# Placing the rows of the last step but one with a selection matrix, and masking the key sums in one instruction, in a four-layer attention kernel

## The chip, the core and the metric

The kernel runs on one core of a Trainium2 chip. A core has five instruction queues that run side by side and meet only at semaphores: TensorE (PE, matrix products into PSUM), VectorE (DVE), ScalarE (ACT), GpSimd (POOL, which here mostly issues DMA transfers) and SyncE (SP, which issues the others). The metric is the device time of one execution in microseconds, the median of the runs. All times below are microseconds unless marked ns.

## What is computed

The reference applies four blocks to a sequence x of 2048 tokens with 512 features, each on a layernorm of x and added back to x: A, B, A, B, with the same weights each time. Cut to what matters:

```python
def A(x, mem):                       # 64 segments of 32 tokens, one after the other
    for s in range(64):
        h = concat([mem, x[32*s:32*s+32]])       # 8 memory rows + 32 tokens
        q, k, v = h @ Wq, h @ Wk, h @ Wv         # 32 heads of 128
        p = softmax(where(mask, q @ k.T * scale, -1e9))
        o = (p @ v) @ Wo
        mem = o[:8]                              # goes into the next segment
        out.append(o[8:])
def B(x):                            # linear attention, 32 heads of 16
    q, k, v = split(x @ wqkv)
    phi = lambda t: where(t > 0, t + 1, exp(t)) + 1e-6
    kv, z = phi(k).T @ v, phi(k).sum(tokens)     # over all 2048 tokens
    return (phi(q) @ kv) / (phi(q) @ z + 1e-6) @ wo
x = x + A(ln(x)); x = x + B(ln(x)); x = x + A(ln(x)); x = x + B(ln(x))
```

A is a recurrence: the 8 memory rows that a segment puts out are an input of the next. B needs the sums kv and z over all tokens before its first output, so the next A layer, or the end of the kernel, waits for the last tokens of the A layer before.

## The kernel before

**Tiles and steps.** Tokens lie in 16 tiles of 128 rows, each covering four segments. A segment is a step; there are 64 steps in a layer, each with its projections (`kq0`, `kq1`, `v`), the memory rows' attention (`mem0`, `mem1`), the product with Wo of the memory rows and the tokens of the step before (`out`, L1386), the memory rows for the next step (`next`) and the tokens' attention (`x`). A step handles 8 memory rows and only the first 24 of its 32 tokens; the last 8 tokens of each of a tile's four segments, 32 rows, are gathered into a fifth block, the left-over rows (`left0` to `lefts`, and `left_rows`, L1443).

**From the output product to x.** `out_proj` leaves the two feature halves of a step's result in the rows of one PSUM tile; two 128-column casts (ACT or DVE, L937 or L938) put part of it into `outW_sb`. `rows_out` (L1432) adds the two partial results into `y_sb` (L1435, DVE, 64x256) and moves the rows to their places in `dx_sb` by DMA, two transfers per group of rows, issued on POOL (L953). When a tile's four steps are there, `residual` (L1447) adds `dx_sb` to x (L1474). For the very last step of a layer (tile 15, g = 3) there is another way: a product with the selection matrix `selz_sb` (L1458, two matmuls) puts the rows of `outW_sb` into place in PSUM, and DVE adds them to x (L1462).

**B, spread over A.** `b_in` (L1545) runs on each finished tile of x: layernorm (L1097 to L1111; ACT does the logarithm and exponential between L1098 and L1103), the products with wqkv, phi (exponential on ACT L1539, then DVE L1540 and L1542), and the sums kv (L1582) and z (L1584). The tokens' x and phi(q) go to scratch in DRAM. After the last tile, `b_mid` (L1599) masks kv to the heads' diagonal blocks (L1604), makes the masked key sums `zf_sb` by four multiplications (L1608), and multiplies kv into wo, in place. `b_out` (L1642) then gives a tile's output: a product with `zf_sb`, reciprocal by logarithm and exponential on ACT (L1667, L1669), a multiplication (L1670), the product with the mixed weights and the addition to x (L1679). In layer 0 tile 0's `b_out` stands ahead of the next A layer's first projection and the others run among its steps; in layer 1 all sixteen stand at the end, and SP stores them.

**The order of the work.** Every operation is recorded with the data that it reads and writes. A table written out in the kernel gives each a number and, where ACT or DVE could do it, the engine: `PERIOD` holds four steps that repeat, `OWN` the steps that differ (the first eleven and the last ones of each layer, the first eight of layer 1, and all of the end). `schedule` (L698) sorts by these numbers, gives out the eight PSUM banks in that order, and derives the semaphore waits. The numbers only set an order; each engine runs its own instructions strictly in it. While PE has nothing to do, `spin` (L1069) has it multiply ones.

## Time and profile before

| what | value |
|---|---|
| three runs, median (lowest to highest) | 1611.34 (1610.76 to 1618.56) |
| the profiled execution | 1611.15 |
| its span | 1609.4 |
| PE busy in the span | 1544.0 (96%) |
| DVE busy | 1221.6 (76%) |
| ACT busy | 1100.0 (68%) |
| POOL busy | 326.8 (20%) |
| granted PE clock, mean | 0.998 |
| first weights there and first projection starts | 25.64 |
| last tile of layer 0: its layernorm starts | 789.11 |
| first projection of layer 1 starts | 805.10 |
| last tile of layer 1: its layernorm starts | 1576.52 |

The span runs from the first to the last record of the trace; the device time also covers what lies around it. An engine's busy time is the sum over its instructions, and instructions of one engine can overlap by some tens of nanoseconds, so that ten DVE operations of 0.68 in a row take 0.60 each on the chain. The chain is followed back from the last instruction, at each step to what released it. "issue" is time in which the engine waited for nothing that the profile shows.

### The profile page before, as it was taken

What the parts mean: (1) busy time and instruction counts of PE and PEld (TensorE: products, weight loads), DVE (VectorE), ACT (ScalarE), POOL (GpSimd) and SP (SyncE); (2) the same over time, 40 slices, a digit from 0 to 9 for tenths busy, and PEclk for the clock granted to TensorE, in tenths of its full rate; (3) what the DMA queues carried; (4) which work ended last, traced back from release to release, by engine and by line L of the source; (5) the groups of instructions that cost most, each with busy time, mean ns of one, the idle gap of its engine ahead of it and who ended that gap; (6) DMA issues with size and microseconds to landing.
All of it is one profiled execution on the core that took longest, in us unless ns stands there. A gap on an engine that the chain in (4) does not pass through costs nothing.

```text
span 1609.4 us, 104163 instructions
## 1 busy us (share of the span) xinstructions
PE 1544.0 (96%) x52074; PEld 882.0 (55%) x43376; DVE 1221.6 (76%) x3899; ACT 1100.0 (68%) x3178; POOL 326.8 (20%) x660
## 2 busy tenths in 40 slices
PE   5899999999999999999999999999999999999997
PEld 1455555555555555555545655556556555555554
DVE  3777777887777787777677778777787877877777
ACT  1567776776776776776467777777777777776665
POOL 2022221122222112222201221222221222221120
PEclk9999999999999999999999999999999999999999
DMA  9300000000000000000000000000000000000013
GB/s 381 104 14 16 14 17 10 16 17 17 17 14 17 10 17 16 17 17 17 25 8 11 17 20 20 20 14 17 21 17 20 21 20 11 21 17 22 24 43 130
DMA packets 35079, 50.96 MB, mean 32 GB/s; under 512 B 13624, under 2 KB 28784, under 8 KB 33104
## 3 DMA queue, kind: packets, MB, share of 16 engines
q0 software_dynamic: 21744, 19.78, 4.3%
q1 hardware_dynamic: 12736, 24.38, 4.1%
q8 instruction: 374, 6.13, 1.6%
q14 instruction: 65, 0.53, 0.1%
q10 hardware_dynamic: 160, 0.14, 0.0%
HBM read 29.63 MB, written 10.49 MB: 25 GB/s over the span
## 4 chain that ended last, share of the span: by engine, by line
PE 85%; DVE 5%; ACT 5%; DMA 2%; issue 1%; POOL 0%; DVEq 0%; SPq 0%
PE pb L1157 27%; PE pb L1053 22%; PE pb L1400 17%; PE pb L1065 11%; ACT arena_sb L937 3%; PE pb L1049 3%; PE pb L1424 2%; DMA Wq_sb<-in_A_Wq_dram 2%; PE pb L1258 2%; DVE arena_sb L938 1%; PE pb L1338 1%; PE pb L1111 1%; DVE st_sb L1097 1%; DMA dx_sb<-y_sb 1%; DVE Wq_sb L1679 1%
## 5 line engine op out<-in xcount | busy, mean ns | idle before, releaser
L937 ACT ACTIVATE arena_sb<-pb 128x512 bf16<-128x512 f32 (+5 forms) x1140 | 521.0, 488 | 273.5 <-PE pb L1053 165.2
L953 POOL DMA_DIRECT2D dx_sb<-y_sb x504 | 254.6, 511 | 1047.7 <-DVE y_sb L1435 822.3
L1157 PE MATMUL pb<-Wk_sb,arena_sb 128*32 128x512 bf16 x4096 | 408.5, 379 | 3.0 <-DVE arena_sb L938 1.4
L1053 PE MATMUL pb<-Wq_sb,arena_sb 128*32 128x512 bf16 x4096 | 408.1, 379 | 0.0
L938 DVE CAST arena_sb<-pb 128x512 bf16<-128x512 f32 (+3 forms) x576 | 311.5, 545 | 110.9 <-PE pb L1053 57.9
L1400 PE MATMUL pb<-Wo_sb,arena_sb 128*32 128x256 bf16 x10368 | 345.3, 273 | 4.3 <-DVE arena_sb L1307 1.7
L1065 PE MATMUL pb<-arena_sb 128*32 128x128 bf16 (+2 forms) x12528 | 321.7, 216 | 4.2 <-ACT arena_sb L937 1.5
L1065 PEld LDWEIGHTS pb<-arena_sb 128*32 128x32 bf16 x12528 | 227.7, 96 | 138.1 <-issue 28.5
L1175 DVE STREAM_TRANSPOSE arena_sb<-arena_sb 128x256 f32<-128x256 f32 x640 | 260.9, 429 | 42.8 <-ACT arena_sb L937 36.6
L1400 PEld LDWEIGHTS pb<-Wo_sb,arena_sb 128*32 128x32 bf16 x10368 | 263.1, 96 | 50.6 <-issue 15.7
L1157 PE MATMUL pb<-Wv_sb,arena_sb 128*32 128x512 bf16 x3248 | 279.6, 378 | 1.1 <-DVE arena_sb L938 1.1
L1157 PEld LDWEIGHTS pb<-Wk_sb,arena_sb 128*32 128x32 bf16 x4096 | 119.4, 96 | 237.5 <-issue 186.2
L1053 PE MATMUL pb<-Wv_sb,arena_sb 128*32 128x512 bf16 x1872 | 202.8, 378 | 0.0
L937 ACT ACTIVATE arena_sb<-arena_sb 32x256 bf16<-32x256 bf16 (+1 forms) x414 | 159.6, 386 | 31.3 <-DVE arena_sb L1345 21.4
L1157 PEld LDWEIGHTS pb<-Wv_sb,arena_sb 128*32 128x32 bf16 x3248 | 95.9, 96 | 73.6 <-issue 19.2
L937 ACT ACTIVATE outW_sb<-pb 128x128 fp32r<-128x128 f32 x317 | 70.3, 273 | 89.2 <-PE pb L1400 86.2
L1307 DVE TENSOR_TENSOR arena_sb<-pb,arena_sb 128x128 bf16<-128x128 f32 x252 | 73.1, 290 | 50.5 <-PE pb L1400 17.2
L1157 PE MATMUL pb<-Wq_sb,arena_sb 128*32 128x512 bf16 x1024 | 101.6, 378 | 4.5 <-DMA Wq_sb<-in_A_Wq_dram 3.4
L1275 ACT ACTIVATE arena_sb<-pb 128x192 bf16<-128x192 f32 (+1 forms) x256 | 83.9, 328 | 31.2 <-PE pb L1258 12.7
L1435 DVE TENSOR_TENSOR y_sb<-pb,outW_sb 64x256 bf16<-64x256 f32 x158 | 65.8, 417 | 47.6 <-ACT outW_sb L937 44.2
L1053 PE MATMUL pb<-Wk_sb,arena_sb 128*32 128x512 bf16 x1024 | 101.7, 378 | 0.0
L1285 DVE TENSOR_TENSOR arena_sb<-arena_sb 128x128 bf16<-128x128 bf16 x504 | 89.0, 215 | 15.9 <-ACT arena_sb L1275 14.1
(109 smaller groups left out, 1793.0 us busy)
## 6 DMA issues: line engine op xcount, KB each, us to landing
Wk_sb<-in_A_Wk_dram SPq DMA_DIRECT2D x1, 4096.0 KB, 13.2
Wq_sb<-in_A_Wq_dram SPq DMA_DIRECT2D x1, 4096.0 KB, 24.3
Wv_sb<-in_A_Wv_dram SPq DMA_DIRECT2D x1, 4096.0 KB, 33.8
Wo_sb<-in_A_Wo_dram SPq DMA_DIRECT2D x16, 256.0 KB, 7.3
xs_scratch<-x_sb POOLq DMA_DIRECT2D x32, 128.0 KB, 2.0
pq_scratch<-arena_sb POOLq DMA_DIRECT2D x32, 128.0 KB, 2.9
dx_sb<-y_sb POOLq DMA_DIRECT2D x252, 12.0 KB, 1.6
dx_sb<-y_sb POOLq DMA_DIRECT2D x252, 4.0 KB, 1.9
```

Of the source, the lines that this page charges most:

```text
L937: return e.activation(o() if callable(o) else o, i() if callable(i) else i, ACTF.Copy)
L938: return e.tensor_copy(o() if callable(o) else o, i() if callable(i) else i)
L953: add(eng, lambda e: e.dma_start(o, i), 0.55 if eng == "pool" else 0.4, reads=reads, writes=writes, dsem="%s%d" % (kind, k), lat=lat + (0. ...
L1053: return pe.add_instruction(mybir.InstMatmult(name=nc.get_next_instruction_name(), engine=mybir.EngineType.PE, ins=[pe.lower_ap(x), pe.low ...
L1065: r = pe.matmul(o[q], w[:, q], x, start=start, stop=stop, skip_group_check=True, tile_position=(0, 32 * j))
L1157: r = pe.matmul(o, blk[:, c, :], w, start=(c == 0), stop=(c == 3), tile_position=(0, 32 * j))
L1175: add("dve", lambda v: v.transpose(dst, src(img[:, k, :].bitcast(F32))), 0.445, reads=[("img", k)], writes=[dkey])
L1275: add("act", lambda a: a.activation(PQ[:, r2, b, 0:nq], tl.f32()[:, 0:nq], ACTF.Exp, scale=SCALE), c_act(nq), tiles=[tl], writes=[("PQ", r ...
L1285: add("dve", lambda v, a=a, p_=p_, w_=w_: v.tensor_tensor(wide(Pm[:, k, a, :]), p_.unsqueeze(2).to_broadcast([128, 4, 4, 8]), w_, ALU.mult ...
L1307: add("dve", lambda v: v.tensor_tensor(oTb[:, s % NO, 16 * b:16 * b + 16, 0:8], pv.f32()[:, 0:128].rearrange("p (n q) -> p n q", q=8), Rm[ ...
L1400: r = pe.matmul(tl.f32()[32 * j:32 * j + 32, 0:256], oT[:, 4 * hh + n, :], Wo_sb[:, 8 * n + hh, 256 * d:256 * d + 256], start=(hh == 0 and ...
L1435: add("dve", lambda v: v.tensor_tensor(y_sb[0:64, k, :], tl.f32()[0:64, 0:256], outW[64:128, w, :].bitcast(F32), ALU.add), c_dve(256), rea ...
```

## The change

Four things change in the code. The selection matrix has four blocks of 32 columns instead of two of 128, made by four more selects in the set-up: two blocks pick a step's rows into places 0 to 31, two skip the 8 memory rows and pick 24 rows into places 0 to 23. The rows of tile 15's last step but one (g = 2) go through a product with it, as those of the last step do, and both additions to x touch 32 rows instead of 128. Since the left-over rows still come through `dx_sb`, POOL first sets its rows 64 to 95 to zero. And the four multiplications of the masked key sums become one with both operands spread out.

```diff
-    selz_sb = sb("selz_sb", [128, 2, 128], F32R)
+    selz_sb = sb("selz_sb", [128, 4, 32], F32R)
...
-        o = 16 + 128 * d
-        sel(scr_sb[q, o + 96:o + 128], ALU.not_equal, 1.0, 0, [[-1, 32]], 1, *SCR)
+        o = 16 + 32 * d
+        sel(scr_sb[q, o:o + 32], ALU.not_equal, 1.0, 0, [[-1, 32]], 1, *SCR)
+        sel(scr_sb[q, o + 64:o + 88], ALU.not_equal, 1.0, -8, [[-1, 24]], 1, *SCR)
...
-            if G == NT - 1 and g == 3:
+            if G == NT - 1 and g == 2:
+                add("pool", lambda p: p.memset(dx_sb[64:96, G % 2, :], 0.0), 0.5, writes=[("dx", G % 2, i, d) for i in (64, 88) for d in range(2)])
+            if G == NT - 1 and g >= 2:
                 tz = P.tile()
+                r = slice(32 * g, 32 * g + 32)
 
                 def pick(pe):
                     for d in range(2):
-                        r = pe.matmul(tz.f32()[:, 256 * d:256 * d + 256], selz_sb[:, d, :], outW[:, w, :], start=d == 0,
+                        u = pe.matmul(tz.f32()[0:32, 256 * d:256 * d + 256], selz_sb[:, d + 6 - 2 * g, :], outW[:, w, :], start=d == 0,
                                       stop=d == 1, skip_group_check=True)
-                    return r
+                    return u
                 add("pe", pick, 0.42, reads=[("outW", w, 0), ("outW", w, 1), "selz"], tiles=[tz], mode=1)
-                add("dve", lambda v: v.tensor_tensor(x, x, tz.f32()[:, :], ALU.add), c_dve(512),
-                    reads=[xk], writes=[xk], tiles=[tz])
-                return
-            rows_out(w, tl, G, [(8, 32 * g, 24)])
+                add("dve", lambda v: v.tensor_tensor(x[r, :], x[r, :], tz.f32()[0:32, :], ALU.add), c_dve(512),
+                    reads=[xk], writes=[xk], tiles=[tz], quad=(g, g))
+                if g == 3:
+                    return
+            else:
+                rows_out(w, tl, G, [(8, 32 * g, 24)])
...
-        for c in range(4):
-            add("dve", lambda v, c=c: v.tensor_scalar_mul(zf_sb[:, c, :], maskbd_sb[:, :], za[:, c:c + 1]), c_dve(128, 2),
-                reads=["za", "maskbd"], writes=["zf"])
+        add("dve", lambda v: v.tensor_tensor(zf_sb[:, :, :], maskbd_sb[:, :].unsqueeze(1).to_broadcast([128, 4, 128]),
+                                             za[:, :].unsqueeze(2).to_broadcast([128, 4, 128]), ALU.mult), c_dve(512),
+            reads=["za", "maskbd"], writes=["zf"])
```

Beside this the table `OWN` is written anew: nearly all of its rows have other numbers, and many operations another engine. `PERIOD` is unchanged. Two of the multiplications of ones load their weights a little less or more often. In the built program the new table moves work in the opening, at the boundary between the layers and at the end. Three of its moves are spoken of below: at layer 0's last tile L1542 stands behind the aggregation of the layernorm (before: ahead of it), at layer 1's last tile all four evacuations of the mixed weights are on DVE (before: three there, one on ACT), and the second tile's tokens are loaded early in the set-up rather than at its end. POOL's order of the other transfers stays.

## Prediction

> **What bounds the kernel now.** I read the page first. Its profiled execution took 1611.15 us with a span of 1609.4, so 1.75 us lie outside the span; the median of the three runs is 1611.34. I work in the span and subtract from the median.

> ```profile
> PE   5899999999999999999999999999999999999997
> PE 85%; DVE 5%; ACT 5%; DMA 2%; issue 1%; POOL 0%; DVEq 0%; SPq 0%
> ```

> The first line (busy tenths in 40 slices) shows PE full from the third slice to the last but one; the second is the chain that ended last, 85% of it matmuls. Little can be gained where PE is full. So I listed, engine by engine, how the two built programs order their instructions. From about 150 to 724 us and from about 897 to 1511 us every engine has the same instructions in the same order in both (PSUM banks only change names). What differs is the opening, the boundary between the layers and the end. I then followed the chain in order of time through both layer ends (start, length, what):

> ```profile
> 784.16 0.52 POOL dx_sb L953
> 784.68 3.00 DMA dx_sb<-y_sb
> ...
> 787.78 0.43 DVE x_sb L1474
> ...
> 788.30 0.69 DVE x_sb L1462
> 788.99 0.20 DVE arena_sb L1540
> 789.19 0.60 DVE st_sb L1097
> 789.79 0.59 DVE arena_sb L1542
> ```
> ```profile
> 1572.54 2.64 DMA dx_sb<-y_sb
> ...
> 1575.28 0.43 DVE x_sb L1474
> ...
> 1575.80 0.70 DVE x_sb L1462
> ...
> 1582.78 0.27 DVE arena_sb L1608
> ```

> In both layers the chain runs through the transfer that is removed, then through the addition of moved rows (L1474) and the product's addition (L1462) into the last layernorm. But what is next late? The timeline of the same places answers (start, length, engine, line):

> ```profile
> 786.50 0.45 ACT L937 ACTIVATE outW_sb<-pb 128x128 fp32r<-128x128 f32 x2 [1.56 <-PE pb L1400]
> 787.04 0.48 PE L1458 MATMUL pb<-outW_sb,selz_sb 128*128 128x256 f32 x2
> 1573.79 0.61 PE L1400 MATMUL pb<-Wo_sb,arena_sb 128*32 128x256 bf16 x14 [0.65 <-issue]
> 1574.95 0.51 PE L1458 MATMUL pb<-outW_sb,selz_sb 128*128 128x256 f32 x2 [0.54 <-ACT outW_sb L937]
> ```

> The last step's selection product is done at 787.52 and 1575.46, hardly before the moved rows (787.68, 1575.18). **Of two transfers of 3.00 and 2.64 us, only 0.74 and 0.30 us are to be had directly**: L1462 could start at about 787.56 instead of 788.30, and 1575.50 instead of 1575.80.

> **The change part by part.**

> *Removed, per layer:* one y addition (L1435, 0.42 us), two transfer issues on POOL (0.51 each) and their wait. *Added, per layer:* two more selection matmuls (0.48 for a pair by L1458, whose moving size of 256 columns stays), one 32x512 addition from PSUM (0.69 by L1462, the same 512 elements a lane) and a POOL memset of 32x512 (about 0.5, an estimate: POOL's 128x272 memset took 0.33, its 128x128 one 0.20). Cover in layer 0: DVE stood idle 3.31 us before L1474, so the addition is free; the memset lies in POOL's idle time. Uncovered, the addition would cost 0.69. The pair of matmuls stands on PE's queue ahead of the last output product (L1400 x64): it waits for the casts of the step before, and behind it wait that product and the whole layer end. In layer 1 PE waited 0.58 us there for an ACT cast, which hides the 0.48.

> *Layer 0, last addition.* 0.74 from above. The new order also puts both 512-wide evacuations ahead of the last output product on DVE (before, one on each of ACT and DVE), with three of the four 32-partition copies on DVE, whose 0.23 us each compares with 0.41 on ACT. That product could then start near 783.9 instead of 784.52. Bound 0 to 0.6, I take 0.4. Sum 1.1.

> *Layer 0, layernorm.* L1542 (0.59) stood between the statistics and their aggregation; it is moved behind the aggregation, beside ACT's two steps (0.30 and 0.21). From the end of L1462 to L1103 it was 2.08 us; the new order needs 0.60+0.20+0.10+0.60 (statistics, L1540, aggregation, then L1542 beside ACT) plus gaps, about 1.55. Gain 0.5.

> *Masked key sums.* Four 128x128 tensor_scalars become one 128x512 tensor_tensor. In layer 1 the four took 1.14 us of the chain (1582.78 to 1583.92). Nearest to the new one is L1604, mask times a float32 tensor: 0.61 on the chain, 0.68 by itself; I take 0.69, gain 0.45. [...] In layer 0 the stretch from L1584 to the end of L1604 took 2.52 us (795.55 to 798.07), with the four, L1582 and L1540 in it; the new order leaves 0.17+0.60+0.64+0.61 and gaps, with L1540 (0.20) behind: gain 0.4.

> *Layer 1, last addition.* 0.30 from above. The stop of 0.65 us inside the output product (1573.14 to 1573.79) has no releaser in the program; should it not come back, 0.95. I take 0.6.

> *Layer 1, tail.* From 1584.6 to 1607.1 DVE is busy 22.42 of 22.50 us: the tail is DVE's. The new order gives DVE all four evacuations of the mixed weights instead of three: 0.6 more. I take -0.5.

> *Opening and steps around the edges.* The first product waits for Wq until 25.64 in either order, and first use of Wv was at 35.93. From 25.6 to 147 us PE idled 121.4 - 113.0 = 8.4 us: the most a new order can regain, while its loss has no bound in the trace. By the durations of the rows the new order reaches step 1's first projection near 49.1 rather than 49.56: I take 0.4, bounds -2 and +2. The four more selects in setup (0.3 each on POOL) end near 16 us; the first product at 25.64 and the first masks near 37 cover them, else 1.2. The earlier load of a 128 KB token tile was issued before Wq's landing in both.

> Sum: 1.1+0.5+0.4 in layer 0, 0.45+0.6-0.5 in layer 1, 0.4 in the opening: 2.95, say 3.0. 1611.34 - 3.0 = **1608.3 us** (span near 1606.4).

> **The rivals.**

> *Another transfer becomes last (0.27).* Six transfers of the left-over rows still feed L1474. In layer 1 their y addition stands about 0.9 us later against the step's key sums than before. Issue takes 6 x 0.5; with the 2.64 to 3.00 us of the chain's transfers rather than the median landing of 1.9, they end as late as the removed ones. Then only the key sums and the layernorm order are gained, 1.4 less 0.2 to 0.5 in the tail: **1610.2**. For it: they were issued until 783.45 and 1570.64, 0.7 and 1.4 us before the removed ones started. Against: in layer 0 they then land by 786.5.

> *Slower: the new matmul pair holds up PE (0.08).* It stands ahead of the last output product and waits for two casts. In layer 0 these are on DVE behind three copies, in layer 1 on ACT behind two copies and a 512-wide evacuation. If they end late, product, evacuation, pick and layernorm all wait. It decides from 1.5 us of waiting at each end, half the gain each. At 2.5 us each, what one step's ACT queue held here (1568.31 to 1570.87), it is 5.0 - 3.0 = 2.0 slower: **1613.3**. Against: DVE was idle 3.31 us here.

> *The order regains idle time too (0.05).* Half of the opening's 8.4 us beside my sum: **1604.1**.

> *Nothing arrives (within the second rival's range):* if all four removed waits are replaced, 1611.

> **How the numbers follow.** My sum 0.60, own range 1606.3 to 1609.8; another transfer 0.27; slower 0.08; more idle time regained 0.05. The range 1603.8 to 1612.3 leaves out most of the slow case and the far edge of the fast one. 0.5%, about 8 us, is what a measurement of this kernel can tell from no change; no case above reaches it on its middle. Faster by more: 0.05, if the opening closes up almost wholly; slower by more: 0.03; within: 0.92.

> **What would show it.** No DMA on the chain at 780 to 790 and at the end; L1462's successor starting 1 us earlier against the step's key sums; one DVE row of 0.6 to 0.7 us for the masked sums; L1103's successor within 1.6 us of the addition; DVE full in the last 22 us; step 1's first projection near 49. Wrong if the pair of selection matmuls sits idle for more than a microsecond ahead of the last output product, if a transfer of the left-over rows ends the wait at L1474's successor, or if PE's idle time to 147 us grows.

## The result, and the profile after

The changed kernel takes 1610.35 us (median of 20 runs, 1605.84 to 1616.08); the kernel before, run beside it, 1612.94 (20 runs). The ratio is 0.9984, with a 95% interval of 0.9977 to 0.9992: 2.6 us faster, between 1.3 and 3.7. So 20 runs of each told 2.6 us from no change, where the forecast held 8 us for the least that can be told. The forecast was 1608.3 from a median of 1611.34, that is 3.0 us faster. So the total came as forecast; of its parts, the layer boundary came, and the end of layer 1 did not.

The page of the changed kernel's profile (span 1606.7), the line that answers to the chain's shares of before, and the line of the queue q8, which by the counts below loads TensorE's instructions:

```profile
PE 87%; ACT 5%; DVE 4%; DMA 2%; issue 1%; POOL 0%; SPq 0%; DVEq 0%; ACTq 0%
q8 instruction: 374, 6.13, 1.6%
```

As a whole the chain is TensorE's, as before. The second line will matter: 374 packets of 16,384 bytes each. TensorE has 52,125 matmuls and 43,379 weight loads in this trace and 344 records of its queue, all but two of them waits: 95,848 in all, 256.3 for each packet (VectorE, the next, has 3,911 instructions). That a packet holds 256 of them, of 64 bytes each, is an estimate from these counts. A packet's worth of instructions is called a block below, and the order in which TensorE's instructions stand its stream.

**Layer 0's end.** The chain of waits in order of time (start, length, what), and below it three VectorE lines of the timeline (start, length, line, shapes, idle time before and what ended it):

```profile
783.03 1.93 PE pb L1401 x64
...
785.51 0.42 PE pb L1462 x2
785.93 0.66 PE pb L1050 x12
786.59 1.53 PE pb L1081 x50
788.12 1.21 PE pb L1054 x46
789.33 0.25 PE pb L1112 x16
```
```profile
784.42 0.42 DVE L1480 TENSOR_TENSOR x_sb<-x_sb,dx_sb 96x512 bf16<-96x512 bf16 x1
785.97 0.68 DVE L1466 TENSOR_TENSOR x_sb<-x_sb,pb 32x512 bf16<-32x512 bf16 x1 [1.13 <-PE pb L1462]
788.28 0.41 DVE L1104 TENSOR_SCALAR arena_sb<-x_sb,st_sb 128x512 bf16<-128x512 bf16 x1
```

No DMA is on the chain any more. The addition of moved rows (L1480) starts without a wait, 1.5 us ahead of the last addition, which now waits for the last selection product. The layernorm ends at 788.69. But the chain doesn't run through it: its transposes (L1112) start at 789.33, behind the filler product of ones (L1081 and the pieces put down to L1054), which holds TensorE until then. Before, they started 0.06 us after the layernorm (its last step and the transposes, from the timeline of before):

```profile
791.07 0.41 DVE L1103 TENSOR_SCALAR arena_sb<-x_sb,st_sb 128x512 bf16<-128x512 bf16 x1 [0.60 <-ACT st_sb L1101]
791.54 0.41 PE L1111 MATMUL pb<-id_sb,arena_sb 128*32 128x128 bf16 x16 [1.29 <-DVE arena_sb L1103]
```

**Layer 1's end.** The chain again:

```profile
1564.58 0.66 PE pb L1401 x24
1565.23 1.58 issue
1566.81 1.30 PE pb L1401 x40
...
1569.12 1.49 PE pb L1401 x46
1570.61 0.27 issue
1570.88 0.74 PE pb L1401 x18
...
1572.19 0.42 PE pb L1462 x2
```

Here too the transfer is gone. In its place TensorE stops twice in the midst of an output product, for 1.58 and 0.27 us, and waits for nothing that the program names. Before had one such stop of 0.65 us on this chain.

The two traces can be compared more closely than by these ends, since with the experiments below there are 14 of them. "Rows of step n" is the moment at which VectorE or ScalarE copies that step's new memory rows into place; LN is the start of the statistics of the layer's last layernorm; key sums is the first addition behind them (L1584 before, L1590 after); the tail runs from layer 1's key sums to VectorE's last instruction. The times are worked out from the instructions' starts in each trace. A star marks a stretch in which TensorE's granted clock was halved for 3.41 us near 1495 (in shifted_stream for 6.83 from 1507; two stars: near 1570 as well). In late_loads and shifted_stream such a piece also lies in the tail.

| trace | start to rows of step 0 | layer 0: rows of 62 to LN | LN to key sums | to the next LN | layer 1: rows of 56 to LN | tail |
|---|---|---|---|---|---|---|
| before | 49.31 | 16.25 | 6.45 | 6.78 | 90.42* | 24.48 |
| before_again | 52.13 | 16.06 | 6.44 | 6.77 | 88.82 | 24.47 |
| opening_only | 50.54 | 16.33 | 6.44 | 6.77 | 88.15 | 24.47 |
| opening_and_boundary | 50.46 | 14.62 | 6.47 | 6.46 | 90.46* | 24.45 |
| edits_in_old_order | 50.65 | 15.76 | 6.44 | 6.56 | 89.77* | 24.03 |
| end_edits_in_old_order | 49.22 | 14.62 | 6.47 | 6.46 | 90.12* | 24.04 |
| changed | 49.14 | 14.62 | 6.47 | 6.46 | 89.60* | 25.13 |
| changed_again | 51.38 | 14.62 | 6.46 | 6.46 | 90.65* | 25.40 |
| counts_of_before | 51.47 | 14.62 | 6.57 | 6.46 | 89.08 | 25.14 |
| short_filler | 50.54 | 14.62 | 6.17 | 6.46 | 87.72 | 25.14 |
| late_loads | 50.33 | 14.62 | 6.47 | 6.46 | 85.89 | 28.00 |
| mixing_evacuation_on_scalar | 51.28 | 14.62 | 6.47 | 6.46 | 91.40** | 25.90 |
| shifted_stream | 48.86 | 14.64 | 6.47 | 6.46 | 92.84* | 26.66 |
| mixed_version | 49.05 | 14.62 | 6.17 | 6.46 | 89.20* | 24.04 |

The boundary's columns repeat to 0.1 us in the new order (the two traces with a shorter filler apart) and to 0.3 in the old one; the first column and the sixth spread by 2 us or more for one and the same order. A difference of single spans (1609.4 and 1606.7) is therefore no measure of this change; the boundary's columns are.

One stretch inside the sixth column is as steady. In layer 1 it took 33.83 or 33.84 us from step 59's rows to step 62's in all six traces with the old order of these steps. With the new order it took 32.58 to 32.85 in six traces, 33.15 in counts_of_before and 33.33 in shifted_stream. So the new order is 0.5 to 1.3 us ahead before the end proper begins.

### The profile page after: what moved, and what is told of

It is laid out like the page before. It is cut to its first block, busy times and chain, and to the rows that moved or that the text cites. A ratio compares the mean times of both kernels' runs of the same rounds, so it can differ in the third digit from the quotient of the medians.

```text
span 1606.7 us, 104210 instructions
## 1 busy us (share of the span) xinstructions
PE 1551.5 (97%) x52125; PEld 882.9 (55%) x43379; DVE 1222.0 (76%) x3911; ACT 1097.5 (68%) x3160; POOL 326.6 (20%) x662
## 2 busy tenths in 40 slices
PE   5899999999999999999999999999999999999997
## 4 chain that ended last, share of the span: by engine, by line
PE 87%; ACT 5%; DVE 4%; DMA 2%; issue 1%; POOL 0%; SPq 0%; DVEq 0%; ACTq 0%
PE pb L1158 27%; PE pb L1054 22%; PE pb L1401 18%; PE pb L1066 11%; PE pb L1050 3%; ACT arena_sb L937 3%; DMA Wv_sb<-in_A_Wv_dram 2%; PE pb L1425 2%; PE pb L1259 2%; PE pb L1339 1%; PE pb L1112 1%; DVE arena_sb L938 1%; DVE st_sb L1098 1%; DVE arena_sb L1286 1%; PE pb L1208 0%
## 5 line engine op out<-in xcount | busy, mean ns | idle before, releaser
L937 ACT ACTIVATE arena_sb<-pb 128x512 bf16<-128x512 f32 (+5 forms) x1150 | 527.8, 490 | 264.3 <-PE pb L1054 168.1
L953 POOL DMA_DIRECT2D dx_sb<-y_sb x500 | 252.8, 512 | 1053.8 <-DVE y_sb L1436 848.9
L1054 PE MATMUL pb<-Wq_sb,arena_sb 128*32 128x512 bf16 x4096 | 407.9, 379 | 0.0
L938 DVE CAST arena_sb<-pb 128x512 bf16<-128x512 f32 (+3 forms) x564 | 303.5, 544 | 105.3 <-PE pb L1054 54.1
L1401 PEld LDWEIGHTS pb<-Wo_sb,arena_sb 128*32 128x32 bf16 x10368 | 263.0, 96 | 48.6 <-issue 15.3
L1054 PE MATMUL pb<-Wv_sb,arena_sb 128*32 128x512 bf16 x1872 | 203.0, 378 | 0.0
L937 ACT ACTIVATE arena_sb<-arena_sb 32x256 bf16<-32x256 bf16 (+1 forms) x400 | 153.8, 385 | 28.6 <-DVE arena_sb L1346 21.6
L937 ACT ACTIVATE outW_sb<-pb 128x128 fp32r<-128x128 f32 x303 | 67.3, 273 | 91.5 <-PE pb L1401 88.3
L1286 DVE TENSOR_TENSOR arena_sb<-arena_sb 128x128 bf16<-128x128 bf16 x504 | 89.8, 215 | 16.6 <-ACT arena_sb L1276 14.8
L1054 PE MATMUL pb<-Wk_sb,arena_sb 128*32 128x512 bf16 x1024 | 101.9, 379 | 0.0
```

Source lines behind the costliest of these rows:

```text
L937: return e.activation(o() if callable(o) else o, i() if callable(i) else i, ACTF.Copy)
L938: return e.tensor_copy(o() if callable(o) else o, i() if callable(i) else i)
L953: add(eng, lambda e: e.dma_start(o, i), 0.55 if eng == "pool" else 0.4, reads=reads, writes=writes, dsem="%s%d" % (kind, k), lat=lat + (0. ...
L1054: return pe.add_instruction(mybir.InstMatmult(name=nc.get_next_instruction_name(), engine=mybir.EngineType.PE, ins=[pe.lower_ap(x), pe.low ...
L1286: add("dve", lambda v, a=a, p_=p_, w_=w_: v.tensor_tensor(wide(Pm[:, k, a, :]), p_.unsqueeze(2).to_broadcast([128, 4, 4, 8]), w_, ALU.mult ...
L1401: r = pe.matmul(tl.f32()[32 * j:32 * j + 32, 0:256], oT[:, 4 * hh + n, :], Wo_sb[:, 8 * n + hh, 256 * d:256 * d + 256], start=(hh == 0 and ...
```

## The experiments

**Which region makes the gain.** The table `OWN` falls into the opening (set-up, steps 0 to 10), the boundary (layer 0's steps 57 to 66, layer 1's steps up to 7) and the end (layer 1 from step 57). Two kernels take the regions in turn from the changed kernel and leave the rest as before.

```diff
 # opening_only: rows of OWN after layer 0's step 10, and SPIN, as before
-            if G == NT - 1 and g == 2:
+            if G == NT - 1 and g == 2 and layer in ():
 # opening_and_boundary: rows of OWN from layer 1's step 57 as before
-            if G == NT - 1 and g == 2:
+            if G == NT - 1 and g == 2 and layer in (0,):
 # both: the four multiplications of b_mid where the edit is off
```

Expected of opening_only:

> Before's kernel with only the opening's new order (set-up and steps 0 to 10 of layer 0, with the four more selects); boundary, end, the two other edits as before. Theory A (the gain is made where the order differs): step 1's first projection near 49.1 as in after, 0.4 us ahead of before, kept to the end, so 0.4 us faster than before in all. Theory B (the 0.4 is a drift of the steps that happens in any run): first projection back near 49.5 and no gain.

Measured: 0.9993 of before (0.9982 to 1.0003). The interval holds 0.4 us and no gain, so neither theory is settled by this. In the trace the granted clock was halved twice in the opening, so that step 0's rows came at 50.54; in the traces whose clock held at 45 us the new order reached them at 48.86 to 49.22 (shifted_stream, changed, mixed_version and end_edits_in_old_order), before at 49.31. By step 12's rows nothing is left of it that could be told: 187.09 in changed, 187.83 in mixed_version, 188.58 in end_edits_in_old_order and 190.62 in shifted_stream, against 187.49 before.

Expected of opening_and_boundary:

> The changed kernel up to layer 1's step 7, with layer 0's edits; the end of layer 1 (steps 57 on, its selection product and its masked key sums) in the order and code of before. Theory A: first projection of layer 1 near 802.4 (before 805.1), 2.4 to 2.9 us faster than before in all if the end's order is worth nothing on balance (after's end gained 1.2 us until step 63's key sums, then lost 0.5 to the last layernorm and 0.65 in the tail). Theory B (the end's edits gain what was forecast, 0.55): at least 0.5 us slower than the changed kernel.

Measured: 1608.16 us, 0.9973 of before (0.9961 to 0.9985), not slower than the whole change (0.9984 and, run again, 0.9979). The intervals overlap too far to exclude theory B's 0.5 us by the times alone, but the stretches speak against it: from step 62's rows to LN 17.12 us here against 17.63 and 18.41, the tail 24.45 against 25.13 and 25.40. With what steps 59 to 62 gain, the end's edits and order bring about nothing on balance. The boundary's stretches are those of the changed kernel to 0.01 us.

**The same kernels again.**

Expected of before_again:

> The kernel before, once more, for a second trace. Every theory: ratio 1.000 within its interval; the layer boundary as in the first trace within 0.2 us (last layernorm of layer 0 at 16.2 to 16.4 us after the step's memory rows), the end of layer 1 too (17.0 to 17.2). Theory A (single times differ by halvings of the clock that come or don't come after short idle times): the opening up to step 0's memory rows differs from the first trace's 49.3 by up to 2 us, and where it does the granted clock is below 1 there.

Measured: 1.0006 (0.9994 to 1.0017); boundary and tail as in the first trace within 0.2 us; the opening 2.8 us longer, with a halved clock from 24.7 to 31.5 us. Theory A's upper figure was too small; the clock was halved where the opening was longer, as it said.

Expected of changed_again:

> The changed kernel once more, unaltered, for a second trace. If TensorE's stop of 1.58 us inside the last output product but one of layer 1 (1565.23 to 1566.81) comes from its instruction supply, which depends on the place in the instruction stream, it comes back at the same matmul, between 1 and 2 us long, and the other stop of 0.27 in the last output product too. If it was a chance event, it is gone and the stretch from step 63's key sums to the last layernorm takes about 8.5 us, not 9.97.

Measured: 0.9979 (0.9969 to 0.9989). Both stops came back in front of the same matmuls, behind 24 of 64 and behind 46 of 64, now 2.08 and 0.55 us long. TensorE's timeline at the first of them:

```profile
1565.66 0.84 PE L1401 MATMUL pb<-Wo_sb,arena_sb 128*32 128x256 bf16 x24
1568.58 1.28 PE L1401 MATMUL pb<-Wo_sb,arena_sb 128*32 128x256 bf16 x40 [2.08 <-issue]
```

So it is no chance event; only its length varies. The opening is 2.2 us longer than in the first trace, and the clock says why. This is the stretch from 24 to 56 us in the first trace, then in the second (stretch, length, busy times of TensorE, its weight loads, VectorE, ScalarE and POOL with their counts, granted clock, DMA share, GB/s).

```profile
24.00:56.00 32.00, 25.27 (x708) 10.26 (x526) 17.59 (x54) 12.68 (x37) 0.78 (x1) 1.00 0.90 324
```
```profile
24.00:56.00 32.00, 25.86 (x620) 10.87 (x450) 15.62 (x47) 11.30 (x32) 0.78 (x1) 0.89 0.90 324
```

The same program in the same order: in the second trace 0.89 of the clock was granted, and TensorE does 88 matmuls fewer in those 32 us.

**The place in the instruction stream.**

```diff
 # shifted_stream
-    SPIN = {(0, 0): (24, 256, 46), (1, 0): (12,), (1, 1): (22, 256, 46), (0, 2): (5,), (0, 3): (7,), (0, 4): (30, 512, 50)}
+    SPIN = {(0, 0): (24, 256, 46), (1, 0): (12,), (1, 1): (22, 256, 46), (0, 2): (5,), (0, 3): (7,), (0, 4): (30, 512, 114)}
 # counts_of_before
-    SPIN = {(0, 0): (24, 256, 46), (1, 0): (12,), (1, 1): (22, 256, 46), (0, 2): (5,), (0, 3): (7,), (0, 4): (30, 512, 50)}
+    SPIN = {(0, 0): (24, 256, 46), (1, 0): (12,), (1, 1): (22, 256, 55), (0, 2): (5,), (0, 3): (7,), (0, 4): (30, 512, 42)}
```

Expected of shifted_stream:

> The changed kernel with 64 more weight loads in the filler product of ones ahead of layer 1's first projection (114 fresh loads, not 50): TensorE's stream of instructions is 64 longer from there on, the work and its order are the same. Theory A (TensorE runs out of instructions at a fixed distance of 256 instructions): the stop that lay after 24 of the 64 matmuls of the last output product but one moves 48 to 64 instructions earlier in the work, to the step's value product or ahead of it, and its length changes, so that the stretch from step 63's key sums to the last layernorm is 0.3 to 1.6 us shorter than 9.97. Theory B (the stop waits for ScalarE's or VectorE's data): same place, same length, 9.97.

Measured: 1626.36 us, 1.0087 of before (1.0074 to 1.0101), four runs: 16 us slower than the changed kernel, 18 than its runs beside this one. The expectation put this filler in the wrong place: it stands in the set-up, ahead of step 0, so the whole stream was shifted. Layer 0 from step 12's rows to step 56's took 519.16 us (515.3 to 517.7 in the other traces), layer 1 from step 8's to step 56's 576.39 (571.1 to 573.6), with the same work in the same order. The stop in the last output product but one was gone from its place; others of 0.5 to 2.0 us stood elsewhere. Theory A holds in that the place in the stream decides, and far beyond the end of a layer. TensorE's idle times put down to "issue" add up to 12.4 us in this trace, against 2.3 in the changed kernel's. About 2.5 of the 12.4 are 16 gaps of 0.16 us at places where the trace lacks records, so some 9.8 us are stops. The clock was halved for 9 us more than in the changed kernel's trace, which is worth 4.5 us at most (an estimate, half of the 9). The rest of the loss stays open. What it means for the change: in the traces without missing records, a period of four steps holds 2,816 records of TensorE in layer 0 and 3,072 in layer 1, its queue's included, 11 and 12 blocks of 256. So every period meets the block ends at the same places, and before_again and the changed kernel reach the repeated steps at the same place in a block. The two changed counts of fresh loads make good what the change adds and removes elsewhere.

Expected of counts_of_before:

> The changed kernel, but the two fillers load their weights as often as before (42 and 55, not 50 and 46): TensorE's stream is 8 instructions shorter through layer 0 and 1 longer through layer 1. Theory A (place in the stream matters, as 64 more instructions cost 18 us): layer 0's 44 steps from 12 to 56, 516 us in five traces and 519.2 with 64 more, take 0.3 to 1.5 us more or less, layer 1's the same. Theory B (only a large shift matters, or none): all within 0.5 us of the changed kernel.

Measured: 0.9992 (0.9982 to 1.0002); layer 0's stretch 516.94, layer 1's 571.71. Theory B: 8 places or 1 place are within the spread of the other traces. The ratio is above the changed kernel's two (0.9984 and 0.9979), but the intervals overlap, so a loss of 1 us or so is not excluded.

**What the filler holds at layer 0's end.**

```diff
-    SPIN = {(0, 0): (24, 256, 46), (1, 0): (12,), (1, 1): (22, 256, 46), (0, 2): (5,), (0, 3): (7,), (0, 4): (30, 512, 50)}
+    SPIN = {(0, 0): (18, 256, 68), (1, 0): (12,), (1, 1): (22, 256, 48), (0, 2): (5,), (0, 3): (7,), (0, 4): (30, 512, 50)}
```

Expected of short_filler:

> The changed kernel with the filler product of ones at layer 0's last layernorm cut from 24 to 18 units (0.65 us of TensorE), its fresh loads raised so that the stream's places hold. Theory A (the filler holds the transposes, 789.33 against the layernorm's end at 788.69): from the layernorm's last step to the key sums 4.88 us becomes 4.25 to 4.5, and everything after it is that much earlier. Theory B (the evacuation and the products behind it are held by something else): 4.88 stays. Theory C: with TensorE idle longer its clock is halved there and the gain is lost.

Measured: 4.58 us (6.17 in the table, from LN on), 0.30 us less instead of 0.4 to 0.6; in time 0.9985 of before (0.9973 to 0.9998), the clock not halved there. Theory A holds, with something else late next. ScalarE's timeline names it:

```profile
793.51 0.60 ACT L1545 ACTIVATE arena_sb<-pb 128x512 bf16<-128x512 f32 x1 [2.62 <-DMA pq_scratch<-arena_sb]
```

The exponential of the last tile writes where the tile before still lies, until a transfer has carried it to DRAM.

**Edits without the new order.**

```diff
 # end_edits_in_old_order: end of layer 1 (OWN) as before, but
-    (1, 63, 'res'): '1599587 1600550 1599644',
+    (1, 63, 'res'): '1539196 1599600 1599650',
 # edits_in_old_order: boundary as before too, SPIN (1, 1) with 51 loads, and
-    (0, 63, 'res'): '819494 820023 820573',
+    (0, 63, 'res'): '768112 819500 819990',
 # in both the masked key sums keep one of their four numbers
```

Expected of end_edits_in_old_order:

> The changed kernel's opening and boundary, and layer 1's end in the order of before, but with both edits: the rows of the last step but one through the selection product, and the masked key sums in one instruction. Theory A (the edits are worth what was forecast for them, and the new order of the end loses it): from step 62's memory rows to the last layernorm 16.4 to 16.9 us (17.0 to 17.2 in three traces with before's order, 17.6 and 18.4 with the new one), the tail from the key sums 23.9 to 24.2 (24.47 before, 25.1 to 25.4 changed); in all about 1 us faster than opening and boundary alone. Theory B (another transfer or the selection product ahead of the last output product takes the gain): 17.0 or more.

Measured: 0.9988 (0.9978 to 0.9999). The tail is 24.04, 0.43 less than 24.47: the key sums in one instruction are worth what was forecast. The last addition came 16.96 us after step 62's rows, hardly earlier than the 17.01 to 17.18 of four traces in the old order: TensorE's stops on the way took 0.91 and 0.11 us here. So theory A holds for the tail; the addition's gain was taken, though by the instruction supply (see late_loads below) and by nothing that theory B names. The whole was not 1 us faster than opening_and_boundary, as was expected: 0.9988 against 0.9973, with overlapping intervals.

Expected of edits_in_old_order:

> The changed kernel's opening; boundary and end in the order of before, but with all three edits in both layers; layer 1's filler loads set (51) so that the stream's places hold. It splits the boundary's gain of 1.72 us between edits and order. Theory A (the edits carry what was forecast for them: 0.74 for the addition, and part of 0.4 for the key sums; the order carries the rest): from step 62's memory rows to layer 0's last layernorm 15.3 to 15.7 us (16.25 before, 14.62 changed), the layernorm's first part 1.97 and the stretch to the key sums 4.48 as before, from the key sums to the next layernorm 6.5 to 6.78 (6.78 before, 6.46 changed). Theory B (the order makes the gain): 16.0 or more in the first stretch. End as in the run before with the edits in the old order: 17.0 and 24.04.

Measured: 0.9979 (0.9969 to 0.999). In layer 0 the selection product alone brings LN at 15.76 us from step 62's rows, 0.3 to 0.6 less than before and between what the two theories expected. But step 62's rows came 0.35 us later than usual, 0.18 of it one "issue" stop at 773.36: from step 56's rows to LN it is 84.91, against 84.82 to 85.14 in the three traces without the edit. Counted from the start of the last output product (786.85 here, 784.52 before, 783.03 in the changed kernel) LN follows after 3.83 us, 4.59 and 3.66: taking the transfer away is worth 0.76, as the direct reading said. But in the old order the product itself starts 0.27 later after step 62's rows, behind the new pair of selection matmuls, and in the new order 0.69 earlier than before. The key sums are worth 0.2 there (6.56). In layer 1 it is 16.52, with stops of 0.36 and 0.23. So the new order makes about 1 us of the boundary's gain (46.86 us from step 62's rows to layer 1's first memory rows here, 45.85 in the changed kernel, 47.38 to 47.63 with neither). The times don't show this: 0.9979 here can't be told from the changed kernel's 0.9984 and 0.9979, since the old order of the end has the shorter tail.

**Why TensorE stops.**

```diff
 # late_loads: SyncE's loads of saved rows wait for the last selection product
-                    after=P.res["Wq"][1] + free, dsem="dl%s%d" % (nm, i), lat=t0 + 0.22 * i)
+                    after=P.res["Wq"][1] + free + [n for n in P.nodes if n.key == (1, NSEG, "res", 0)], dsem="dl%s%d" % (nm, i), lat=t0 + 0.22 * i)
```

Expected of late_loads:

> The changed kernel, but the loads of the saved rows for the last sixteen outputs (issued from 1560 on by SyncE) wait for the last selection product of layer 1. Theory A (TensorE's instruction blocks come late in the last output product but one because these loads hold the DMA engines: the block fetched at 1564.19 began 2.56 us after TensorE had entered the block before, others 0.1 to 1.9): that delay falls to 1.1 to 1.6 us, the stop from 1.6 to 2.1 us falls below 0.6, and from step 62's memory rows to the last layernorm it takes 16.2 to 16.8 us, not 17.4 to 18.4. Theory B (the stop comes from the density of the instructions alone): the stop stays above 1.2 us. Both: the tail gets longer by 1 to 8 us, since the outputs wait for the loads.

Measured: 0.9978 (0.9968 to 0.9989). From step 62's rows to LN 15.65 us (17.63 in the changed kernel), the shortest of all, with no stop. The timeline of TensorE (start, length, line, shapes, count):

```profile
1563.66 1.94 PE L1401 MATMUL pb<-Wo_sb,arena_sb 128*32 128x256 bf16 x64
...
1566.51 0.42 PE L1462 MATMUL pb<-outW_sb,selz_sb 128*32 128x256 f32 x2
1566.94 1.93 PE L1401 MATMUL pb<-Wo_sb,arena_sb 128*32 128x256 bf16 x64
```

Both output products run through. And the DMA engines (columns as above, the last but one their busy share) while the block was fetched, first in the changed kernel, then here:

```profile
1563.80:1565.60 1.80, 1.43 (x40) 0.83 (x29) 1.67 (x8) 1.77 (x5) 0.81 (x3) 1.00 0.99 315
```
```profile
1561.00:1562.80 1.80, 1.80 (x101) 1.69 (x90) 1.48 (x5) 0.50 (x2) 0.24 (x1) 1.00 0.03 9
```

0.99 against 0.03. In the packets of the instruction queue: in the changed kernel TensorE enters a block at 1561.63, the next block's packet starts 2.56 us later and takes 1.05, and TensorE goes on 1.57 after that. With late loads the packet starts 0.47 us after the block is entered (1560.90, 1561.37) and is there long before it is needed. Theory A holds, by more than it expected (1.1 to 1.6 us to the packet, 16.2 to 16.8 to LN); the same dense products without the loads had no stop, so theory B falls. The loads took the fault with them: they now run from 1569.92 on, and a block entered at 1575.27 had to wait 3.90 us for the next packet to start, with the DMA engines moving 371 GB/s in between. There a stop of 2.08 us stands at 1579.71, followed by a piece of halved clock. The tail takes 28.00, and the time is the same as the changed kernel's.

**The tail.**

```diff
 # mixing_evacuation_on_scalar
-    (1, 66, 'bm'): '1610539 1609120 1612340 1612965v 1612556 1614178v 1612751 1613733v 1611282 1611752v',
+    (1, 66, 'bm'): '1610539 1609120 1612340 1612965v 1612556 1614178a 1612751 1613733v 1611282 1611752v',
```

Expected of mixing_evacuation_on_scalar:

> The changed kernel with one of layer 1's four evacuations of the mixed weights moved from VectorE to ScalarE, as before had it. Theory A (the tail is VectorE's work laid end to end): from the key sums to VectorE's last instruction 24.4 to 24.6 us instead of 25.13. Theory B (ScalarE's logarithms and exponentials bound the tail's first 11 us, as the chain of the changed kernel says): 25.1 or more.

Measured: 0.9983 (0.9971 to 0.9996), tail 25.90 with a stop of 0.38 in it. Theory A falls: taking the 0.6 us off VectorE didn't shorten the tail, which is 25.52 less its stop, against 25.13. (An evacuation is a copy out of PSUM.) The changed kernel's chain there, abridged, and two VectorE lines of its timeline:

```profile
1582.93 0.69 ACT Wk_sb L1673
...
1593.54 0.69 DVE Wq_sb L1676
```
```profile
1579.62 0.69 DVE L1613 TENSOR_TENSOR arena_sb<-maskbd_sb,arena_sb 128x512 bf16<-128x512 bf16 x1
1582.71 0.69 DVE L938 CAST arena_sb<-pb 128x512 bf16<-128x512 f32 x1 [0.39 <-PE pb L1066]
```

Until 1593.5 the chain is ScalarE's logarithms and exponentials, back to back, and VectorE stood idle 0.39 us for the first mixed weights. So in the new order the tail isn't VectorE's work alone: ScalarE sets its first 11 us.

**Put together.** The changed kernel's opening, boundary and steps 57 to 62, the shorter filler, and from step 63 of layer 1 on the order of before with both edits.

```diff
 # from step 63 of layer 1 on OWN as before, but
-    (1, 63, 'res'): '1599587 1600550 1599644',
+    (1, 63, 'res'): '1539196 1599600 1599650',
-    SPIN = {(0, 0): (24, 256, 46), (1, 0): (12,), (1, 1): (22, 256, 46), (0, 2): (5,), (0, 3): (7,), (0, 4): (30, 512, 50)}
+    SPIN = {(0, 0): (18, 256, 68), (1, 0): (12,), (1, 1): (22, 256, 48), (0, 2): (5,), (0, 3): (7,), (0, 4): (30, 512, 50)}
```

Expected of mixed_version:

> What the runs point to, put together: the changed kernel's opening, boundary and steps 57 to 62 of layer 1, the shorter filler (18 units, more loads), and from step 63 of layer 1 on the order of before with both edits. By the parts: 0.30 (filler), 0.4 to 1.4 (last addition of layer 1) and 1.1 (tail) faster than the changed kernel in the trace, less 0.17 after the last addition: 1.6 to 2.6 us, so near 0.9970 of before. Rival (the steps ahead set where the block of instructions ends, and the stop comes back as long as before in the last output product but one): no faster than the changed kernel beyond the tail's 1.1.

Measured: 1606.85 us, 0.9963 of before (0.995 to 0.9976), the fastest of all; the changed kernel had 0.9979 and 0.9984, so it is 2.6 or 3.4 us ahead of it, at or above the expected 1.6 to 2.6, with intervals that overlap (seven runs). By the stretches the filler gives 0.30 and the tail 1.09, as expected. The last addition gives 0.33 from step 62's rows, less than the expected 0.4 to 1.4: the stops were only 0.35 and 0.23, but without them it still took 16.72 us, against 15.9 in the two traces with the edits in the old order. At the seam of the two orders the chain leaves TensorE for VectorE and ScalarE from 1560.24 to 1562.43, which it doesn't do in end_edits_in_old_order.

## Why the prediction was right in sum, step by step

- *Layer 0, last addition* (forecast 1.1). 1.6: 16.06 to 16.33 became 14.62. Its two terms: 0.74 direct (0.76 with the edit alone, 0.93 with the new order), and an earlier start of the last output product, sized 0.4 within 0 to 0.6, measured 0.69 after step 62's rows. The mechanism held, the sizes were low. Without the new order the second term is a loss of 0.27: there the chain runs through the new pair of selection matmuls into the output product, which is the second rival's mechanism in small.
- *Layer 0, layernorm* (0.5). The layernorm became 0.38 shorter (1.97 to 1.59), and nothing of it arrives: LN to key sums is 6.45 and 6.47. The step that failed is "gain 0.5" itself: the stretch was summed as if its end were the bound, and what is next late was not asked. The filler of 24 units is as long as before, and its end became the bound; after it, by short_filler, the transfer of phi(q).
- *Layer 0, key sums* (0.4). 0.32: 6.78 to 6.46, 0.2 of it the edit alone.
- *Key sums in layer 1* (0.45). 0.43, in the old order. The one instruction takes 0.69 in both layers, as the row for the mask of kv said; the four took 1.14. The range also set aside 0.2 for a loss by the merge; no run shows one, the two with the edit in the old order gained 0.43 (end_edits_in_old_order, layer 1) and 0.2 (edits_in_old_order, layer 0).
- *Layer 1, last addition* (0.6). The direct gain is there, and TensorE's stops took it. Subtracting the stops, step 62's rows to LN took 16.3 to 16.6 us in four traces of the old order without the edit (before: 17.18 - 0.65 - 0.09), 15.93 and 15.94 with it, and 15.8 in four traces of the new order (changed: 17.63 - 1.58 - 0.27; changed_again: 18.41 - 2.08 - 0.55), 15.65 in late_loads, which has no stop: 0.5 to 0.8 gained. With the stops these four traces of the new order took 17.36 to 18.41, against 17.01 to 17.18. The step that failed is "should it not come back": the stop of 0.65 seen before was put down as something that may go, half of it was booked as gain, and it came back as 1.6 to 2.4 us in the five traces that keep the new end, its loads and the stream in its place. Why it is so long, late_loads shows: the block's packet waits behind the loads of the saved rows (it started 2.56 us after the block before was entered in the changed kernel and 0.47 after with the loads later; over the time of that block the DMA engines were 0.98 and 0.13 busy).
- *Layer 1, tail* (-0.5 beside the key sums' 0.45, so about nothing). -0.65: 24.48 to 25.13. With the edit but the old order it is 24.04, so the new order loses 1.09, not the 0.5 that was booked. The step that failed is "the tail is DVE's": the fourth evacuation was to cost its 0.6 there, but giving it back to ScalarE (mixing_evacuation_on_scalar) gained nothing, and ScalarE sets the first 11 us. 0.39 of the loss is VectorE's idle time for the mixed weights; which of the new tail's moves loses the rest stays open.
- *Opening* (0.4). Where the clock held at 45 us, 0.1 to 0.45 earlier at step 0's rows (48.86 to 49.22 against 49.31); step 1's first projection at 49.39 instead of 49.56, 0.17 earlier and not the 0.4 of the forecast, and by step 12's rows even the sign is open. TensorE's idle time from 25.6 to 147 us went from 8.4 to 7.7 (before_again 7.3; 5.9 to 8.4 in the traces with the new opening), so the rival that regains half of it didn't come. A halving of the clock near 45 us, in 8 of the 14 traces, costs 1.2 to 1.5 us (3.41 long) or 2.1 to 2.3 (6.83). It was seen in 8 of 12 traces of the new opening and in neither of the two of the old one, of which before_again had another at 25 us. Over whole executions the new opening loses no clock: the granted clock was 0.9976 in the mean of 106 runs of before, and 0.9977 in 48 runs of the four kernels with the new opening and the old order of the end.
- *Rivals.* Another transfer last: no; L1480 starts without a wait in both layers. The selection products ahead of the last output product: in the changed kernel they ran at 782.37 and 1568.63, and the product then waited for an evacuation that ended just before it (on VectorE from 782.28 to 782.99, the product at 783.03; on ScalarE from 1568.58 to 1569.08, the product at 1569.12). In layer 1 TensorE was held ahead of that product, but by its instruction supply, which no rival named.
- *Steps 59 to 62 of layer 1* (nothing forecast). The new order gained 0.5 to 1.3 there, 1.25 in the first trace. The forecast followed the chain only behind these steps and had no term for them.

So the gain that can be shown is the boundary's: from the rows of step 62 to layer 1's first memory rows it took 47.38 to 47.63 us and takes 45.85 in the changed kernel (45.55 to 45.96 in every trace with the new order there), about 1.7 less, where 2.0 were forecast. In layer 1, from step 59's rows to LN it took 50.85 to 51.02 in the four traces with the old end and takes 50.21 and 51.19 in the changed kernel's two, whose tails lose 0.65 and 0.93. The opening shows nothing that can be told. So these stretches add up to 1.8 us in one trace and 0.5 in the other, at the lower end of the measured 1.3 to 3.7 and below it; where the rest comes from isn't shown. That the total came so close to the forecast's 3.0 is in part luck: gains that were forecast and didn't arrive (0.5 at the layernorm, 0.6 at the last addition of layer 1, 0.4 in the opening) stand against one that nobody forecast, and the measured 2.6 is itself known only to 1.2 either way.

## What to carry to other kernels

When an order written by hand takes a wait away, look at once at what else has a fixed length there: a filler sized to the old wait gives the gain back. Before a stretch of dense small matmuls is tightened, look at its "issue" time and at the bulk loads beside it: here a stream that by estimate needed a new block of instructions every 3.5 us stopped for up to 2.44 us while loads filled the DMA engines (0.98 busy in the changed kernel's trace). And compare stretches between the same two instructions, not spans: here the boundary's stretches repeat to 0.1 us, the spans to 3.
